# Softmax attention with one head's scores in two halves of 256 queries, and another owner order of the PSUM banks

## The chip, the cores and the metric

The kernel runs on one core of a Trainium2 chip. The metric is the time of one execution in device microseconds (us); shorter is better. PE is the matmul engine (PEld its weight loads), ACT the engine of exponentials and copies, DVE and POOL the vector engines, SP the engine whose queue issues the DMAs.

## The reference

Two attentions over the same 2048 tokens of width 448, 16 heads of 28 each, mixed by a gate. `a` is a linear attention with a learned feature map; `b` is plain softmax attention, and the change lies in `b`:

```
g = sigmoid((x * gate_w).sum(-1))
phi = concat(softmax(p), softmax(-p)) of p = q @ w_phi and k @ w_phi
a = (phi_q (phi_k^T v)) / (phi_q (phi_k^T 1) + 1e-6) @ wo_a
scores = einsum("bhqd,bhkd->bhqk", q, k) * 28**-0.5
b = softmax(scores) @ v @ wo_b
out = g * a + (1 - g) * b
```

All inputs and outputs are float32.

## The kernel before

The first 360 us or so make the projections, all of `a`, and the row maxima of the first queries. Then the softmax attention runs in steps. A step `s` is one group of four heads (of 4 groups), one block of 512 queries (of 4) and one tile of 128 keys (of 16): 256 steps, the first of which is made earlier (`first_scores`). The loop at the end of the kernel calls `scores(s, ...)` and then `values(s - 2)`: the value matmuls of a step come two steps after its scores.

A head has 28 rows of q and k, so four heads lie in four row groups of 32 of PE's array, and matmuls of different heads may run side by side. The operands are kept as a high and a low part, and a score tile of 128 keys by 512 queries is the sum of three passes (`PASSES`, `score`): high by high, low by high, high by low. One of the spare rows of the operands carries the row maximum of the query, so that the exponential of the tile is already the shifted one.

The row maxima of later queries are found ahead, three in a step (`mx_next`, 704 in all): `mx_score` makes a plain score tile of 128 queries by 512 keys of one head, and `mx_done` lets DVE reduce it to a maximum per query. `todo` is the list of these three; its fourth column is the head. In the step's own list l0 and l1 are the heads of the first two, and e0 and e1 the two others, in an order that the third row maximum sets.

Each score tile and each row maximum's tile takes one PSUM bank. Seven banks (`free`) go round: a step with three row maxima takes all seven, four for scores (`st`) and three for maxima (`pm`), and the list `free` is left in the order in which the next step will take them. A bank's next writer on PE waits until ACT (for scores) or DVE (for maxima) has read it. The eighth bank (`pv`) collects the values.

Engines work their instructions in the written order. PE's order in a step of before is, by rounds: e0, e1, maximum of l0, maximum of l1; e0, e1, l0, l1; e0, e1, l0, l1; l0, l1; third maximum, which uses e0's row group; then eight value matmuls (L975). ACT makes four exponentials of 512 columns (L838) in the order e0, e1, l0, l1, each into its own tile of 16 (four steps' worth). DVE makes three reductions (L295).

Of the kernel before, what the change touches and what calls it, by code (L numbers as in the profile page):

```python
# [8 lines left out]
F32 = mybir.dt.float32  # L9
F32R = mybir.dt.float32r  # L10
U32 = mybir.dt.uint32
AF = mybir.ActivationFunctionType
# [5 lines left out]
P = 128  # L18
# [7 lines left out]
NQ = S // 512  # L26
SCALE = DH ** -0.5
# [14 lines left out]
def gated_mix_kernel(ctx, tc, xT, wqkB, wvB, wvA, wkAT, wqAT, phi, woA, woB,  # L42
# [7 lines left out]
    nc = tc.nc  # L50
# [18 lines left out]
    def ps_mx(nm):  # L69
        return ps.tile([P, 512], F32, tag="mx", name=nm, bufs=psn[1])  # L70
# [214 lines left out]
    def mx_score(item, pm):  # L285
        gq, kb, qt, j, _ = item
        js = slice(32 * j, 32 * j + DH)
        nc.tensor.matmul(pm, mxs[("qc", gq)][js, qt * P:(qt + 1) * P],  # L288
                         mxs[("kc", gq // NQ, kb)][js, :], start=True, stop=True,
                         tile_position=(32 * j, 0))  # L290

    def mx_done(item, pm):
        gq, kb, qt, h, col = item
        g, qb = divmod(gq, NQ)
        nc.vector.tensor_reduce(part[:, col:col + 1], pm, AX.X, ALU.max)  # L295
        if h < 3:
            return
        if kb == 1 and qt == 0 and gq + 1 < NG * NQ:
            mx_query(gq + 1)
        if qb == NQ - 1 and g + 1 < NG:  # L300
            if qt == 2 and kb == 3:
                mx_load(g + 1, 0)
            if qt == 3 and kb < 3:
                mx_load(g + 1, kb + 1)
        if qt == 3 and kb == 3:
            mx_reduce(gq)
# [374 lines left out]
    for i in range(2 * NT + 11):  # L681
        t, q = i, i - NT
# [106 lines left out]
    at = ctx.enter_context(tc.tile_pool(name="at", bufs=1, side="right", reuse_waits="tile"))  # L789
    qst_of, kst_of = {}, {}  # L790
# [31 lines left out]
    pv_of, pts, late, mids = {}, {}, {}, {}  # L822
    PASSES = ((0, 0), (1, 0), (0, 1))

    def score(s, j, n, st):

        gq, kt = divmod(s, NT)
        k, q = PASSES[n]
        js = slice(32 * j, 32 * j + 32)
        nc.tensor.matmul(st[j], kst_of[(gq // NQ, kt // 4)][js, k, (kt % 4) * P:(kt % 4 + 1) * P],  # L830
                         qst_of[gq][js, q, :], start=n == 0, stop=n == 2,
                         tile_position=(32 * j, 0), skip_group_check=True)

    def exps_of(s, js, st, pool, **kw):
        pts[s] = {}
        for j in js:
            p = pts[s][j] = pool.tile([P, 512], F32, name=f"p{s}_{j}", **kw)
            nc.scalar.activation(p, st[j], AF.Exp, scale=SCALE)  # L838

    def first_scores():  # L840
        st = [ps_mx(f"st0_{j}") for j in range(4)]
        for n in range(3):
            for j in range(4):
                score(0, j, n, st)
        exps_of(0, range(4), st, at)

    def scores(s, todo):

        if len(todo) == 3:
            l0, l1, e0 = [x[3] for x in todo]
            e1, = {0, 1, 2, 3} - {l0, l1, e0}
            b = free[:]
            free[:] = [b[2], b[0], b[3], b[1], b[6], b[4], b[5]]
            b = [bank(i, f"g{s}_{n}") for n, i in enumerate(b)]
            st, pm = {e0: b[0], e1: b[1], l0: b[4], l1: b[5]}, [b[2], b[3], b[6]]
            for n in range(4):
                for j in (e0, e1) if n < 3 else ():
                    score(s, j, n, st)  # L860
                for i, j in enumerate((l0, l1)):
                    if n:
                        score(s, j, n - 1, st)
                    else:
                        mx_score(todo[i], pm[i])
            mx_score(todo[2], pm[2])
            js = (e0, e1, l0, l1)
        else:
            js = range(4)
            n = 4 + len(todo)  # L870
            b = free[:n]
            free[:] = free[n:] + b[4:] + b[:4]
            b = [bank(i, f"g{s}_{n}") for n, i in enumerate(b)]
            st, pm = dict(enumerate(b[:4])), b[4:]
            for n in range(3):
                for j in js:
                    score(s, j, n, st)
            for x, m in zip(todo, pm):
                mx_score(x, m)
        exps_of(s, js, st, late_p, tag="p", bufs=16)  # L880
        for x, m in zip(todo, pm):
            mx_done(x, m)
# [10 lines left out]
    for t in range(8, NT):  # L893


        if t < NT - 1:
            value_b(t, lambda i: mx_unit() if (11 * (t - 8) + i + 1) * rest // 77
                    > (11 * (t - 8) + i) * rest // 77 else None)
        else:
            value_b(t, lambda i: first_scores() if i == 4 else None)  # L900
        take_acts()
        if t in (8, 12):
            load_k(0, t // 12)
# [10 lines left out]
    free = [0, 1, 2, 3, 4, 5, 6]  # L914

    def bank(i, nm):
        return ps2.tile([P, 512], F32, tag=f"g{i}", name=nm, bufs=1)
# [187 lines left out]
    for s in range(NS + 18):  # L1105
        gq, kt = divmod(s, NT)
# [17 lines left out]
        if 0 < s < NS:  # L1124
            if s in mids:
                mids.pop(s)()
            scores(s, mx_next())
# [83 lines left out]
```

## Time and profile before

| what | before |
|---|---|
| median of 3 runs | 987.37 us (986.72 to 989.15) |
| the profiled execution | 986.75 us |
| its span in the trace | 985.0 us |
| PE, ACT, DVE busy | 99%, 76%, 74% |
| PE's granted clock | full all through |

A row of a group has the line, the engine, the operation, output and input tile by the program's names with their shapes, and the count; behind the bar the busy time in us and the mean of one in ns; behind the second bar the engine's idle time just before such instructions and what ended it. A row of the timeline has the start and the length in us, then the same names; equal neighbours are merged, so that the length runs from the first one's start to the last one's end. Matmul ends are modelled and instructions of one engine overlap, so starts are the safer numbers. Timeline rows were asked for in narrow windows where single instructions were wanted; a merged row then begins with the first instruction that reaches into the window.

### The profile page before, as it was taken

To read this page: it belongs to the slowest core of one execution; us is meant where nothing else is said; L and a number is where in the kernel's file an instruction comes from. 1 tells how busy PE (TensorE), PEld (TensorE's weight loads), DVE (VectorE), ACT (ScalarE), POOL (GpSimd) and SP (SyncE) were. 2 spreads that over 40 slices of the span, in tenths; PEclk is the share of its full clock that TensorE was granted. 3 is DMA by queue.
4 is the path that set the end of the run, shared out by engine and by line. 5 is a ranking of instruction groups with operands and counts; after the bars stand their busy time and mean duration, and the time that the engine had idled before them with its cause. 6 is when DMAs were issued, how large, how long until landed. Compare 5 with 4: busy or idle time off the path is not lost.

```text
span 985.0 us, 22282 instructions
## 1 busy us (share of the span) xinstructions
PE 979.2 (99%) x8392; PEld 607.2 (62%) x8392; DVE 728.5 (74%) x1335; ACT 752.9 (76%) x1442; POOL 234.8 (24%) x224
## 2 busy tenths in 40 slices
PE   9999999999999999999999999999999999999998
PEld 8877877887777665555555555555555555555555
DVE  5566767899766678888888888888888888885112
ACT  4455655577775689988988988988888898897561
POOL 1135535578734710031011001011001011000010
PEclk9999999999999999999999999999999999999999
DMA  9873010013233233121132121122231223000451
GB/s 304 310 253 116 33 54 32 36 37 98 79 103 112 90 114 127 37 58 46 65 89 73 35 61 48 57 82 71 61 83 50 60 58 84 22 20 31 132 159 57
DMA packets 56140, 84.47 MB, mean 86 GB/s; under 512 B 17217, under 2 KB 23985, under 8 KB 56033
## 3 DMA queue, kind: packets, MB, share of 16 engines
q1 hardware_dynamic: 56032, 83.06, 27.3%
q8 instruction: 66, 1.08, 0.5%
q14 instruction: 42, 0.34, 0.1%
HBM read 54.86 MB, written 27.78 MB: 84 GB/s over the span
## 4 chain that ended last, share of the span: by engine, by line
PE 95%; DVE 3%; issue 1%; ACT 0%; POOL 0%; DVEq 0%; POOLq 0%; ACTq 0%
PE g L830 29%; PE pv L975 26%; PE pqk L109 6%; PE poa L109 4%; PE pk L127 4%; PE pva L127 4%; PE g L288 3%; PE pmd L260 3%; PE pob L109 3%; PE pvb L127 2%; PE pvb L109 2%; PE pq L109 2%; PE pn L507 1%; PE pqk L608 1%; PE pft L495 1%
## 5 line engine op out<-in xcount | busy, mean ns | idle before, releaser
L838 ACT ACTIVATE p<-g 128x512 f32<-128x512 f32 x1020 | 526.1, 607 | 83.9 <-PE g L830 83.1
L295 DVE TENSOR_REDUCE part<-g 128x1 f32<-128x512 f32 x704 | 442.3, 684 | 84.4 <-PE g L288 80.4
L830 PEld LDWEIGHTS g<-qst,kst 32*128 32x128 f32 x3060 | 221.2, 183 | 212.1 <-DVE part L295 194.6
L830 PE MATMUL g<-qst,kst 32*128 32x512 f32 x3060 | 337.9, 420 | 0.1
L975 PE MATMUL pv<-p,vb 128*32 128x512 f32 x2048 | 273.0, 605 | 0.0
L288 PE MATMUL g<-kc,qc 28*128 28x512 f32 x704 | 233.3, 495 | 0.0
L394 POOL TENSOR_TENSOR oUb<-oUb,rsb 128x512 f32<-128x512 f32 x15 | 19.3, 1286 | 490.5 <-DMA rsb<-rdb 458.4
L265 DVE CUSTOM_DVE_ANT_0 rl<-pmb,rl 128x512 f32<-128x512 f32 x160 | 103.2, 682 | 44.0 <-ACT rl L264 44.0
L264 ACT ACTIVATE rl<-pmd 128x512 f32<-128x512 f32 x160 | 87.3, 601 | 31.2 <-PE pmb L260 30.0
L288 PEld LDWEIGHTS g<-kc,qc 28*128 28x128 f32 x704 | 86.5, 182 | 0.2
L975 PEld LDWEIGHTS pv<-p,vb 128*32 128x32 f32 x2048 | 40.7, 108 | 65.9 <-issue 64.6
L109 PE MATMUL pqk<-XH,wB 128*128 128x512 f32 x192 | 59.1, 397 | 0.0
L986 DVE SCALAR_TENSOR_TENSOR acc<-pob,gate,acc 128x448 f32<-128x448 f32 x12 | 8.2, 684 | 54.7 <-PE pob L109 54.7
L546 ACT CAST ev<-pqk 128x512 fp32r<-128x512 f32 x28 | 16.0, 589 | 39.5 <-PE pqk L109 23.0
L109 PE MATMUL poa<-woA_s,oTa 128*128 128x448 f32 x192 | 43.5, 375 | 0.0
L260 PE MATMUL pmb<-kp,qp 28*128 28x512 f32 x160 | 42.1, 496 | 0.4
L547 DVE TENSOR_TENSOR ev<-pqk,ev 128x512 fp32r<-128x512 f32 x28 | 19.0, 690 | 30.9 <-ACT ev L546 30.8
L109 PEld LDWEIGHTS pqk<-XH,wB 128*128 128x128 f32 x192 | 35.5, 188 | 8.5 <-issue 1.5
L260 PE MATMUL pmd<-kp,qp 28*128 28x512 f32 x160 | 39.9, 494 | 0.0
L127 PE MATMUL pk<-wkA_s,XH 128*128 128x448 f32 x128 | 39.4, 382 | 0.0
L109 PEld LDWEIGHTS poa<-woA_s,oTa 128*128 128x128 f32 x192 | 35.0, 189 | 6.3 <-issue 2.9
L127 PE MATMUL pva<-wvA_s,XH 128*128 128x450 f32 x128 | 37.8, 372 | 0.0
(154 smaller groups left out, 1089.2 us busy)
## 6 DMA issues: line engine op xcount, KB each, us to landing
qkd<-ev SPq DMA_DIRECT2D x28, 512.0 KB
qst<-qkd SPq DMA_DIRECT2D x64, 112.0 KB
kst<-qkd SPq DMA_DIRECT2D x64, 112.0 KB
od<-oTb SPq DMA_DIRECT2D x48, 112.0 KB
rsa<-rda SPq DMA_DIRECT2D x8, 512.0 KB
oL<-od SPq DMA_DIRECT2D x8, 512.0 KB
rsb<-rdb SPq DMA_DIRECT2D x15, 256.0 KB
gad<-ga SPq DMA_DIRECT2D x16, 224.0 KB
```

Source lines behind the costliest of these rows:

```text
L109: nc.tensor.matmul(dst, l, r, start=i == 0, stop=i == len(todo) - 1)
L127: nc.tensor.matmul(dst[:, :n], l, r, start=i == 0, stop=i == len(todo) - 1, skip_group_check=True)
L260: nc.tensor.matmul(pm[j], qc[js, qt * P:(qt + 1) * P], kc[js, :], start=True, stop=True, tile_position=(32 * i, 0))
L264: nc.scalar.activation(rl, pm[i], AF.Relu)
L265: nc.vector.tensor_tensor_reduce(rl, pm[2 + i], rl, 1.0, LOWEST, ALU.add, ALU.max, part[:, col + i:col + i + 1])
L288: nc.tensor.matmul(pm, mxs[("qc", gq)][js, qt * P:(qt + 1) * P], mxs[("kc", gq // NQ, kb)][js, :], start=True, stop=True, tile_position=(3 ...
L295: nc.vector.tensor_reduce(part[:, col:col + 1], pm, AX.X, ALU.max)
L394: (nc.gpsimd if n == 1 else nc.vector).tensor_mul(oU, oU, rs)
L547: nc.vector.tensor_sub(e[:, 1, :], pq, f32(e[:, 0, :]))
L830: nc.tensor.matmul(st[j], kst_of[(gq // NQ, kt // 4)][js, k, (kt % 4) * P:(kt % 4 + 1) * P], qst_of[gq][js, q, :], start=n == 0, stop=n == ...
L838: nc.scalar.activation(p, st[j], AF.Exp, scale=SCALE)
L975: nc.tensor.matmul(pv[32 * j:32 * j + 32, :], vb[kt // 8][:, kt % 8, 4 * g + j, :], pt[j], start=kt == 0, stop=kt == NT - 1, tile_position ...
```

## The change

In each step with three row maxima, the scores of e0 are made and exponentiated in two halves of 256 queries: six passes of 256 columns instead of three of 512, two exponentials of 256 instead of one. Both halves lie in one bank and one output tile. PE's order is rewritten around them. The third row maximum now uses e1's row group, so e0 and e1 change names in the first two lines. ACT's order becomes first half of e0, e1, second half of e0, l0, l1. The list `free` leaves the banks in another order: e0 takes the bank of the first row maximum, e1 that of e1, the first two maxima those of the second maximum and of e0, l0 that of l0, l1 that of the third maximum, and the third maximum that of l1. Before, the order was: e0 from the first maximum, e1 from e0, the first two maxima from the second maximum and e1, l0 from the third maximum, l1 from l0, the third maximum from l1. Steps with fewer than three row maxima, and the first one, keep their four whole heads.

```diff
-    def score(s, j, n, st):
+    def score(s, j, n, st, c=slice(0, 512)):
...
-        nc.tensor.matmul(st[j], kst_of[(gq // NQ, kt // 4)][js, k, (kt % 4) * P:(kt % 4 + 1) * P],
-                         qst_of[gq][js, q, :], start=n == 0, stop=n == 2,
+        nc.tensor.matmul(st[j][:, c], kst_of[(gq // NQ, kt // 4)][js, k, (kt % 4) * P:(kt % 4 + 1) * P],
+                         qst_of[gq][js, q, c], start=n == 0, stop=n == 2,
                          tile_position=(32 * j, 0), skip_group_check=True)
     def exps_of(s, js, st, pool, **kw):
         pts[s] = {}
-        for j in js:
-            p = pts[s][j] = pool.tile([P, 512], F32, name=f"p{s}_{j}", **kw)
-            nc.scalar.activation(p, st[j], AF.Exp, scale=SCALE)
+        for j, c in js:
+            if j not in pts[s]:
+                pts[s][j] = pool.tile([P, 512], F32, name=f"p{s}_{j}", **kw)
+            nc.scalar.activation(pts[s][j][:, c], st[j][:, c], AF.Exp, scale=SCALE)
+
+    HALF = slice(0, 256), slice(256, 512)
+
+    def whole(js):
+        return [(j, slice(0, 512)) for j in js]
...
         if len(todo) == 3:
-            l0, l1, e0 = [x[3] for x in todo]
-            e1, = {0, 1, 2, 3} - {l0, l1, e0}
+            l0, l1, e1 = [x[3] for x in todo]
+            e0, = {0, 1, 2, 3} - {l0, l1, e1}
             b = free[:]
-            free[:] = [b[2], b[0], b[3], b[1], b[6], b[4], b[5]]
+            free[:] = [b[2], b[1], b[3], b[0], b[4], b[6], b[5]]
             b = [bank(i, f"g{s}_{n}") for n, i in enumerate(b)]
             st, pm = {e0: b[0], e1: b[1], l0: b[4], l1: b[5]}, [b[2], b[3], b[6]]
-            for n in range(4):
-                for j in (e0, e1) if n < 3 else ():
-                    score(s, j, n, st)
-                for i, j in enumerate((l0, l1)):
-                    if n:
-                        score(s, j, n - 1, st)
-                    else:
-                        mx_score(todo[i], pm[i])
+            score(s, e0, 0, st, HALF[0])
+            score(s, e1, 0, st)
+            mx_score(todo[0], pm[0])
+            mx_score(todo[1], pm[1])
+            score(s, e0, 1, st, HALF[0])
+            for j, n in ((e1, 1), (l0, 0), (l1, 0)):
+                score(s, j, n, st)
+            score(s, e0, 2, st, HALF[0])
+            score(s, e0, 0, st, HALF[1])
+            for j, n in ((e1, 2), (l0, 1), (l1, 1)):
+                score(s, j, n, st)
+            score(s, e0, 1, st, HALF[1])
+            score(s, e0, 2, st, HALF[1])
+            for j in (l0, l1):
+                score(s, j, 2, st)
             mx_score(todo[2], pm[2])
-            js = (e0, e1, l0, l1)
+            js = [(e0, HALF[0])] + whole([e1]) + [(e0, HALF[1])] + whole([l0, l1])
```

More of the change, by code (lines that the diff above doesn't have):

```diff
@@ L844, in first_scores @@
                 score(0, j, n, st)
-        exps_of(0, range(4), st, at)
+        exps_of(0, whole(range(4)), st, at)
     def scores(s, todo):
         if len(todo) == 3:
-            l0, l1, e0 = [x[3] for x in todo]
-            e1, = {0, 1, 2, 3} - {l0, l1, e0}
+            l0, l1, e1 = [x[3] for x in todo]
+            e0, = {0, 1, 2, 3} - {l0, l1, e1}
             b = free[:]
-            free[:] = [b[2], b[0], b[3], b[1], b[6], b[4], b[5]]
+            free[:] = [b[2], b[1], b[3], b[0], b[4], b[6], b[5]]
             b = [bank(i, f"g{s}_{n}") for n, i in enumerate(b)]
             st, pm = {e0: b[0], e1: b[1], l0: b[4], l1: b[5]}, [b[2], b[3], b[6]]
-            for n in range(4):
-                for j in (e0, e1) if n < 3 else ():
-                    score(s, j, n, st)
-                for i, j in enumerate((l0, l1)):
-                    if n:
-                        score(s, j, n - 1, st)
-                    else:
-                        mx_score(todo[i], pm[i])
+            score(s, e0, 0, st, HALF[0])
[13 more added lines that the diff above has]
+                score(s, j, 2, st)
             mx_score(todo[2], pm[2])
-            js = (e0, e1, l0, l1)
+            js = [(e0, HALF[0])] + whole([e1]) + [(e0, HALF[1])] + whole([l0, l1])
         else:
@@ L879, in scores @@
                 mx_score(x, m)
+            js = whole(js)
         exps_of(s, js, st, late_p, tag="p", bufs=16)
```

## The prediction

> **What bounds the kernel now.** I read the page's totals first, then the attention stretch 400 to 900 us by groups and by waits, then one step instruction by instruction.
>
> ```profile
> PE 979.2 (99%) x8392; PEld 607.2 (62%) x8392; DVE 728.5 (74%) x1335; ACT 752.9 (76%) x1442; POOL 234.8 (24%) x224
> ...
> L838 ACT ACTIVATE p<-g 128x512 f32<-128x512 f32 x870 | 449.4, 604 | 51.3 <-PE g L830 50.8 <-PE g L288 0.5
> L295 DVE TENSOR_REDUCE part<-g 128x1 f32<-128x512 f32 x651 | 409.1, 684 | 76.1 <-PE g L288 72.2 <-PE g L830 3.9
> L830 PE MATMUL g<-qst,kst 32*128 32x512 f32 x2610 | 294.1, 419 | 0.0
> ```
>
> A busy PE at 99% says little, since the ends of matmuls are modelled. The counts say more: 2610 score matmuls at 12 a step are 217.5 steps in 500 us, so **2.30 us a step**. ACT waits 51 us of these 500 us for scores, so ACT alone is not the bound either. One step:
>
> ```profile
> 664.65 0.50 PE L830 MATMUL g<-qst,kst 32*128 32x512 f32 x2
> 664.66 0.50 PE L288 MATMUL g<-kc,qc 28*128 28x512 f32 x2
> 665.00 0.51 PE L830 MATMUL g<-qst,kst 32*128 32x512 f32 x4
> 665.23 0.63 PE L830 MATMUL g<-qst,kst 32*128 32x512 f32 x5
> 665.26 1.89 DVE L295 TENSOR_REDUCE part<-g 128x1 f32<-128x512 f32 x3 [0.45 <-PE g L288]
> 665.72 2.06 ACT L838 ACTIVATE p<-g 128x512 f32<-128x512 f32 x4 [0.27 <-PE g L830]
> 665.93 0.64 PE L975 MATMUL pv<-p,vb 128*32 128x512 f32 x4
> ...
> 666.69 0.60 ACT L838 ACTIVATE p<-g 128x512 f32<-128x512 f32 x1
> 666.93 0.50 PE L830 MATMUL g<-qst,kst 32*128 32x512 f32 x2
> 667.27 0.43 PE L830 MATMUL g<-qst,kst 32*128 32x512 f32 x3
> 667.35 0.73 PE L830 MATMUL g<-qst,kst 32*128 32x512 f32 x5
> 667.91 0.39 PE L830 MATMUL g<-qst,kst 32*128 32x512 f32 x1
> 668.26 0.64 PE L975 MATMUL pv<-p,vb 128*32 128x512 f32 x4
> ```
>
> Four heads sit in four row groups and run side by side, so matmuls come in rounds of four: 664.65, 665.00, 665.23. The first round takes 0.34 us, because its weights are loaded with nothing to hide them (0.50 us for one, against 0.39 later); a following round in the same row groups takes 0.23. The third round of e0 and e1 starts at 665.23 and their exponentials at 665.72, 0.49 later. ACT starts one every 0.48 us ((2.06 less 0.61) / 3). The third exponential, that of l0, starts at 666.69 and ends at 667.29; 0.06 later, at 667.35, the first pass of l1 of the next step starts, in the bank that l0 left. It could have started at 667.27, with its round. So l1's chain is 0.08 late: its third pass stands at 667.91, the value matmuls 0.35 later at 668.26, and values take 1.00 (665.93 to 666.93).
>
> The loop: from a step's start to its first exponential 1.07, to l0's exponential 0.97, its length 0.60, release 0.06; in the next step two more passes of l1 0.56, to the values 0.35, values 1.00. That is 4.61 for two steps, **2.30 a step**, the mean above. With no bank late, a fourth round would start 0.23 after 665.23 and the values 0.35 later: 0.58 + 0.23 + 0.35 + 1.00 = 2.16 a step.
>
> **What the change does, and what it does not.** In the changed kernel as built, PE counts its finished work up, and ACT waits for a count. For step 61 the program holds this (mx: row maximum; p0 to p2: the three passes; h0, h1: the halves of e0):
>
> ```
> PE   mx l0 +1 = 3347; mx l1 +1 = 3348
> PE   h0p1 e1p1 l0p0 l1p0 h0p2 h1p0 e1p2 l0p1 l1p1 h1p1: no count
> PE   h1p2 +11 = 3359; l0p2 +1 = 3360; l1p2 +1 = 3361; mx e1 +1 = 3362
> ACT  exp h0 waits 3359; exp e1, exp h1: no wait for PE; exp l0 waits 3360; exp l1 waits 3361
> PE   next step: h0p0 waits for row maximum 1, e1p0 for exp e1, mx l0 for row maximum 2,
>      mx l1 for exp h1, l0p0 for exp l0, l1p0 for row maximum 3, mx e1 for exp l1
> ```
>
> Exp h0 reads columns 0 to 255, ready after h0p2, but it waits for h1p2, the last write into that bank. **The early start isn't there**: h0, e1 and h1 all become free to run together. What is left is a fifth exponential, six short passes for three long ones, and new owners of the banks.
>
> The Trainium skill, "PSUM — Partial Sum Buffer", section "PSUM bank collisions raise a hardware error", says the same from the other side: TensorE may not write a bank while ScalarE reads it, in the same partitions, even at other columns. By that rule no order of these halves could start h0 early while h1 is still written; no run here shows it, and the sum goes by the counts.
>
> **The cost, part by part.** ACT first. No exponential of 256 columns is in the trace; the nearest is a copy of that size out of PSUM:
>
> ```profile
> 277.00 0.39 ACT L498 COPY fT<-pft 112x256 f32<-112x256 f32 x1
> 277.26 0.63 ACT L264 ACTIVATE rl<-pmd 128x512 f32<-128x512 f32 x1
> ...
> L498 ACT COPY fT<-pft 112x512 f32<-112x512 f32 x28 | 15.1, 599 | 0.0
> ...
> L838 ACT ACTIVATE p<-g 128x512 f32<-128x512 f32 x1020 | 526.1, 607 | 83.9 <-PE g L830 83.1
> ```
>
> The next instruction starts 0.26 after it. Bounds: 0.24 (half of 0.48) to 0.39 (no overlap). I take 0.26, since the full-size copies and exponentials agree too (599 ns and 607 ns). So ACT runs h0 0.26, e1 0.48, h1 0.26, and l0 starts 1.00 after h0 instead of 0.97. With its length 0.60 and release 0.06, l0's bank comes free 1.66 after exp h0 starts.
>
> Now PE. Before, l0's bank went to l1 and the first pass of l1 stood behind e0p1 and e1p1; l1 ran on by itself, and e0 was hardly touched. After, l0's bank goes to l0p0, which now waits for the *fourth* exponential. Behind it in PE's order stand l1p0, h0p2, h1p0, e1p2 and the rest: two thirds of e0's work. In the old kernel's case of 667.35 e0 and e1 still had their second passes running. What a held PE costs shows in another step, where the wait was long:
>
> ```profile
> 602.95 0.19 PEld L830 LDWEIGHTS g<-qst,kst 32*128 32x128 f32 x4 [0.24 <-ACT p L838]
> 602.95 0.51 PE L830 MATMUL g<-qst,kst 32*128 32x512 f32 x4
> 603.28 0.41 PE L830 MATMUL g<-qst,kst 32*128 32x512 f32 x2
> 603.55 0.60 ACT L838 ACTIVATE p<-g 128x512 f32<-128x512 f32 x1 [0.16 <-PE g L830]
> ```
>
> No weights are loaded past the held instruction; all four load after the release, so the round takes 0.34 (602.95 to 603.28) and e0's exponential comes 0.60 after its pass instead of 0.49: 0.11 for the bare weight load.
>
> A short pass: by columns 0.12 (half of 0.23), with the next weights loaded behind it. Its floor by loads is seen in matmuls of 128 columns that load 128 columns of weights each:
>
> ```profile
> L1072 PE MATMUL pr<-ident,rw x8: 275/276/377, 973.5 to 974.4; 128*128 128x128 f32 x8
> ...
> 973.80 0.83 PE L1072 MATMUL pr<-ident,rw 128*128 128x128 f32 x6
> ...
> L830 PEld LDWEIGHTS g<-qst,kst 32*128 32x128 f32 x3060 | 221.2, 183 | 212.1 <-DVE part L295 194.6
> ```
>
> At 276 ns for one, (0.83 - 0.28) / 5 = 0.11 from start to start, so a load hides in 0.11. Bounds for a short pass: 0.12 to 0.18 (the recorded length of a weight load, 183 ns). I take 0.12.
>
> From the release R of l0p0: h0p2's weights 0.11, h0p2 streams to 0.23, h1p0 to 0.35. h1p1 stands behind l0p1 and l1p1, which follow l0p0 and l1p0 by 0.34, so h1p1 starts at 0.35 and h1p2 at 0.46. Exp h0 follows a pass of e0 by 0.49 less the 0.12 that this pass is shorter, 0.37: R + 0.84 (0.46 + 0.37, rounded at the end). The loop now closes in a single step:
>
> exp h0 to release 1.66 + release to the next exp h0 0.84 = **2.50 us a step**, 0.20 more than 2.30.
>
> The other limits lie under it. The values follow l1p2 and mx e1 (R + 0.58) by 0.35 and take 1.00, so the next step starts at R + 1.93 and could want l0's bank 0.34 later, at R + 2.27; it comes at R + 2.50. Mx l1 waits for exp h1, free at R + 2.03 (0.84, 0.26 + 0.48, 0.39 for its length, 0.06): 0.10 after the step's start, but 0.47 ahead of the next R, so it costs nothing. Mx e1 waits for exp l1, R + 0.84 + 1.66 + 0.48 = R + 2.98, that is 0.48 after the new R, earlier than its place at 0.58. The third row maximum comes about 0.6 before l1p0 needs it: mx e1 at 0.58, DVE's start 0.60 later (as 664.66 to 665.26), 0.68 for the reduction: R + 1.86. Taking e1 for e0 in it moves one of four passes from one row group to the other, and no DMA: the row maxima keep their order in time, and so do SP's issues. Values of a step read exponentials of two steps earlier, which hides the later end of l1.
>
> ```profile
> L295 DVE TENSOR_REDUCE part<-g 128x1 f32<-128x512 f32 x704 | 442.3, 684 | 84.4 <-PE g L288 80.4 <-PE g L830 3.9
> ```
>
> 704 row maxima in threes make 234 changed steps. 234 x 0.20 = **47 us**. The profiled execution took 986.75 us (span 985.0 and 1.75 around it), 0.6 under the median of the three runs. 985.0 + 47 is a span of 1032; against the median it is 987.4 + 46.8 = **1034 us**.
>
> **The rivals.**
> *The held weights cost nothing* (14%): if h0p2's weights are in place before the release, the chain is 0.11 shorter and the step 2.40: 234 x 0.10 = 23, 1010 us. With a half exponential at 0.24 it would be 2.36, 1001. Against it stand the four loads at 602.95.
> *Short passes of one row group do not overlap their weights* (8%). At 0.18 each, h1p2 starts at R + 0.66, the step is 2.69, 1078 us; with load and pass wholly in line, 0.11 + 0.12 = 0.23 each, h1p2 starts at R + 0.79, 2.82, 1109. Against it: 665.00 to 665.23 is 0.23 in the same row groups, a new load included, where a bare load would make it the 0.34 of the first round. The Trainium skill, "TensorE: Matmul & The Clock Gate", section "The mechanism", states that rule: a weight load overlaps running matmuls only in another row group. This trace disagrees with it by that 0.23.
> *Faster* (5%): exp h0 does start after h0p2. Then ACT is ahead by some 0.3, no bank is late, and PE's own 2.16 decides: 234 x 0.14 = 33 less, 955 us. For it: ACT's 51 us of waiting for scores. Against: the count of 3359.
> *No change* (4%): the swap of banks ends the old loop, and the new one closes in 2.30 as well. The way from R to exp h0 would have to be 0.64 instead of 0.84, so that even four short passes in 0.06 each wouldn't do without the first rival.
>
> **How the numbers follow.** The forecast has 69%, with its own range 1022 to 1050 (0.15 to 0.27 a step: a few hundredths on each of two half exponentials and four short passes). Adding the first rival and part of the way to the second gives 1006 to 1064. About 0.3% (3 us) is what can be told from no change here: faster 5%, within 4%, slower 91%.
>
> **What would show it.** In 400 to 900 us: about 200 steps instead of 217, so 400 exponentials of 256 columns and 600 of 512; the weight loads before l0p0 waiting for ACT some 0.2 a step; four loads together right after that wait; exp h0 0.37 after h1p2, never after h0p2; three exponentials in a row without a gap 0.26, 0.48, 0.26 apart; DVE's share down in proportion to the step. Wrong would be: exp h0 starting while h1's passes run, half exponentials 0.3 or more apart, short passes more than 0.14 apart in one row group, or PE's wait for ACT at another place than l0p0.

## The result, and the profile after

The changed kernel takes 1045.26 us (median of 4 runs, 1044.06 to 1045.8) against 987.46 before: a ratio of 1.0581, 95% interval 1.0563 to 1.0599, 58 us slower. Its profiled execution spans 1042.3 us, 57.3 more than before's 985.0.

From the profile of after, the page's totals:

```profile
PE 1036.1 (99%) x9094; PEld 598.2 (57%) x9094; DVE 729.2 (70%) x1335; ACT 767.4 (74%) x1676; POOL 234.6 (23%) x224
```

The groups of the stretch 400 to 900 us, shapes kept apart:

```profile
L839 ACT ACTIVATE p<-g 128x512 f32<-128x512 f32 x589 | 334.0, 614 | 0.0
L839 ACT ACTIVATE p<-g 128x256 f32<-128x256 f32 x392 | 152.0, 388 | 82.3 <-PE g L830 82.3
L830 PE MATMUL g<-qst,kst 32*128 32x512 f32 x1769 | 315.0, 436 | 0.0
L830 PE MATMUL g<-qst,kst 32*128 32x256 f32 x1180 | 248.5, 316 | 0.0
```

The waits of the same stretch (who waited for whom: us in total, times, the longest):

```profile
ACT p L839 <- PE g L830: 82.3, 196, 0.5
PEld g L830 <- ACT p L839: 59.5, 197, 0.3
```

392 half exponentials are 196 steps in 500 us: 2.55 us a step, where before made 217.5 steps of 2.30. PE's weight loads wait 59.5 us for ACT, once a step, 0.30 each; ACT waits 82.3 us for PE, where before it waited 50.8, and its share of the span falls from 76% to 74% with 234 instructions more. Each waits for the other: that is what a closed loop looks like.

One step of after, put together from narrow windows of the timeline (starts are what counts):

```profile
665.59 0.38 ACT L839 ACTIVATE p<-g 128x256 f32<-128x256 f32 x1 [0.43 <-PE g L830]
665.87 0.59 ACT L839 ACTIVATE p<-g 128x512 f32<-128x512 f32 x1
666.35 0.39 ACT L839 ACTIVATE p<-g 128x256 f32<-128x256 f32 x1
666.61 0.62 ACT L839 ACTIVATE p<-g 128x512 f32<-128x512 f32 x1
667.28 0.20 PEld L830 LDWEIGHTS g<-qst,kst 32*128 32x128 f32 x4 [0.30 <-ACT p L839]
667.29 0.51 PE L830 MATMUL g<-qst,kst 32*128 32x512 f32 x4
667.76 0.27 PE L830 MATMUL g<-qst,kst 32*128 32x256 f32 x1
668.13 0.38 ACT L839 ACTIVATE p<-g 128x256 f32<-128x256 f32 x1 [0.41 <-PE g L830]
```

Exp h0, e1, h1 and l0 start 0.28, 0.48 and 0.26 apart. l0's ends at 667.23 (666.61 + 0.62); 0.05 later PE, which has loaded no weights for 0.30, loads four sets at once. The last short pass of e0, h1p2, starts at 667.76, and the next exp h0 at 668.13, 0.37 behind it. From exp h0 to exp h0 are 2.54 us: 1.64 to the end of exp l0, 0.05 release, 0.47 to h1p2, 0.37 to ACT (each rounded).

### The profile page after: what moved, and what is told of

It is laid out like the page before. It is cut to its first block, busy times and chain, and to the rows that moved or that the text cites. A ratio compares the mean times of both kernels' runs of the same rounds, so it can differ in the third digit from the quotient of the medians.

```text
span 1042.3 us, 23748 instructions
## 1 busy us (share of the span) xinstructions
PE 1036.1 (99%) x9094; PEld 598.2 (57%) x9094; DVE 729.2 (70%) x1335; ACT 767.4 (74%) x1676; POOL 234.6 (23%) x224
## 4 chain that ended last, share of the span: by engine, by line
PE 92%; DVE 3%; DMA 2%; issue 1%; ACT 1%; SPq 0%; DVEq 0%; ACTq 0%
PE g L830 31%; PE pv L989 25%; PE g L288 5%; PE poa L109 4%; PE pqk L109 4%; PE pk L127 4%; PE pva L127 4%; PE pmd L260 3%; PE pob L109 3%; PE pvb L127 2%; PE pvb L109 2%; PE pq L109 2%; PE pn L507 1%; DMA xraw<-in_xT_dram 1%; DMA qkd<-ev 1%; PE pft L495 1%
## 5 line engine op out<-in xcount | busy, mean ns | idle before, releaser
L839 ACT ACTIVATE p<-g 128x256 f32<-128x256 f32 (+1 forms) x1254 | 540.8, 532 | 126.6 <-PE g L830 125.8
L830 PE MATMUL g<-qst,kst 32*128 32x512 f32 (+1 forms) x3762 | 397.1, 391 | 0.4 <-ACT p L839 0.3
L830 PEld LDWEIGHTS g<-qst,kst 32*128 32x128 f32 x3762 | 217.1, 183 | 278.1 <-DVE part L295 192.4
L288 PE MATMUL g<-kc,qc 28*128 28x512 f32 x704 | 264.4, 494 | 0.0
L288 PEld LDWEIGHTS g<-kc,qc 28*128 28x128 f32 x704 | 117.7, 182 | 0.2
```

The source lines that it names most:

```text
L830: nc.tensor.matmul(st[j][:, c], kst_of[(gq // NQ, kt // 4)][js, k, (kt % 4) * P:(kt % 4 + 1) * P], qst_of[gq][js, q, c], start=n == 0, sto ...
L839: nc.scalar.activation(pts[s][j][:, c], st[j][:, c], AF.Exp, scale=SCALE)
```

## The experiments

All are compared with the kernel before, run on the same chip beside them (986.5 to 987.1 us). Where nothing else is said, the diff is against the changed kernel.

**Halves taken out, banks kept.** PE's list has three whole passes of e0 at the places of its first passes, and ACT one exponential.

```diff
-            score(s, e0, 0, st, HALF[0])
+            score(s, e0, 0, st)
...
-            score(s, e0, 1, st, HALF[0])
+            score(s, e0, 1, st)
...
-            score(s, e0, 2, st, HALF[0])
-            score(s, e0, 0, st, HALF[1])
+            score(s, e0, 2, st)
...
-            score(s, e0, 1, st, HALF[1])
-            score(s, e0, 2, st, HALF[1])
...
-            js = [(e0, HALF[0])] + whole([e1]) + [(e0, HALF[1])] + whole([l0, l1])
+            js = whole((e0, e1, l0, l1))
```

> Nothing is halved: e0 has three passes of 512 columns and one exponential again; the new order of the banks and the third row maximum on e1's rows stay. Theory (the loss is the single-step loop: l0's first pass waits for ACT, and e0's short passes stand behind it): with whole heads l0's exponential is the third again and frees the bank about 1.63 us after exp e0 starts; e0's third pass follows l0's first at once, so that the next exp e0 comes 0.60 after the release. 2.23 closes below 2.30, and the two-step loop of before decides again, through l0's three passes in place of l1's: 1.07 + 1.63 + 0.57 + 0.35 + 1.00 = 4.62 for two steps, 2.31 a step, 987 to 991 us. Rival (the new order of the banks is what costs): most of the loss stays, 1030 us or more.

988.53 us, ratio 1.0013 (1.0004 to 1.0022). The new order of the banks and the third row maximum on e1's rows cost 1.5 us between them. The loss is in the halves.

**The banks' order of before, halves kept.**

```diff
-            free[:] = [b[2], b[1], b[3], b[0], b[4], b[6], b[5]]
+            free[:] = [b[2], b[0], b[3], b[1], b[6], b[4], b[5]]
```

> The changed kernel with the banks' order of before (l0 takes the third row maximum's bank, l1 that of l0, e1 that of e0). Theory: l1's first pass now waits for exp l0, and it stands one place behind l0's first pass, with the same four short passes of e0 behind it: the same loop of 1.69 + 0.84 = 2.53 to 2.55 a step, 1040 to 1048 us. Rival (the banks' order costs): back to about 990 us.

1040.69 us, ratio 1.0541 (1.0524 to 1.0559). Now l1's first pass waits for exp l0, with the same four short passes behind it, and nearly the same time comes out, 4.6 us less than with the new order. So it is not the bank as such: whichever first pass waits for exp l0, what stands behind that wait decides. Its waits from 400 to 900 us show PE and ACT waiting for each other once a step:

```profile
ACT p L839 <- PE g L830: 79.5, 197, 0.4
...
PEld g L830 <- ACT p L839: 37.0, 190, 0.2
```

**Short passes, but one whole exponential.**

```diff
-            js = [(e0, HALF[0])] + whole([e1]) + [(e0, HALF[1])] + whole([l0, l1])
+            js = whole((e0, e1, l0, l1))
```

> The changed kernel with its six short passes, but one whole exponential of e0 (four exponentials a step). Theory: exp e0 to the release of l0's bank is 0.06 shorter (1.63 for 1.69), release to the next exp e0 stays 0.84: 2.48 to 2.49 a step, 1029 to 1032 us. So the short passes behind the wait make four fifths of the loss. Rival (the fifth exponential is the loss, ACT being the busiest engine by its own count): back to 990 us.

1030.1 us, ratio 1.0432 (1.0416 to 1.0448). Three quarters of the loss stay without the fifth exponential. So does the wait once a step, PE's part of it at 0.20 each (400 to 900 us):

```profile
ACT p L839 <- PE g L830: 83.8, 200, 0.5
...
PEld g L830 <- ACT p L839: 38.6, 195, 0.2
```

**Whole passes, but two half exponentials**: the passes of the first experiment with the `js` of the changed kernel.

> The changed kernel with whole passes of e0 on PE and its two half exponentials on ACT (both wait for the third pass). Theory: one whole pass stands behind the wait, so the single-step loop is 1.69 + 0.60 = 2.29 and doesn't decide; the two-step loop through l0's three passes is 1.07 + 1.69 + 0.57 + 0.35 + 1.00 = 4.68, 2.34 a step: 993 to 1000 us. Rival (the fifth exponential is a large part of the loss by itself): above 1010 us.

996.49 us, ratio 1.0087 (1.0071 to 1.0103). With the four kernels the two parts can be read as a square (medians in us):

| e0's passes on PE | one exponential of e0 | two halves |
|---|---|---|
| three whole | 988.5 | 996.5 |
| six short | 1030.1 | 1045.3 |

The second exponential costs 8 us beside whole passes and 15 beside short ones; the short passes cost 42 and 49. Beside whole passes the two-step loop decides, which has the added ACT time once in two steps; beside short ones the loop closes in one step and has it in each. The 8 and the 15 fit that factor of two: 234 steps times 0.06, the time added by the two halves, are 14 us. The loop beside whole passes was added up but not followed in its trace.

**Two more short passes ahead of l0's first pass.** Nothing is taken away.

```diff
             score(s, e0, 1, st, HALF[0])
-            for j, n in ((e1, 1), (l0, 0), (l1, 0)):
-                score(s, j, n, st)
+            score(s, e1, 1, st)
             score(s, e0, 2, st, HALF[0])
             score(s, e0, 0, st, HALF[1])
-            for j, n in ((e1, 2), (l0, 1), (l1, 1)):
-                score(s, j, n, st)
+            score(s, l0, 0, st)
+            score(s, l1, 0, st)
             score(s, e0, 1, st, HALF[1])
             score(s, e0, 2, st, HALF[1])
+            for j, n in ((e1, 2), (l0, 1), (l1, 1)):
+                score(s, j, n, st)
```

> The changed kernel with its halves, but two more short passes (third pass of the first half, first pass of the second) issued ahead of l0's first pass, so that two and not four stand behind the wait for exp l0. Theory: release to the next exp h0 falls from 0.84 to about 0.61, that loop to 2.30; the two-step loop through l0's three passes is then 1.07 + 1.69 + 0.57 + 0.35 + 1.00 = 4.68, 2.34 a step: 993 to 1003 us, three quarters of the loss gone with no work taken away. Rival (the extra work itself, short passes and a fifth exponential, costs): no change, 1040 us or more.

997.48 us, ratio 1.0106 (1.0088 to 1.0125). The same instructions in another order on PE give back 48 of the 58 us, to within 1 us of the kernel with whole passes and two exponentials. So the short passes cost next to nothing as work; they cost because they stand behind a wait for ACT. Of the waits from 400 to 900 us, PE's for ACT is gone, and ACT's for PE is down to:

```profile
ACT p L839 <- PE g L830: 45.4, 213, 0.5
```

**All short passes ahead.** e1p2 and all six short passes stand ahead of l0's first pass.

```diff
             score(s, e0, 1, st, HALF[0])
-            for j, n in ((e1, 1), (l0, 0), (l1, 0)):
-                score(s, j, n, st)
+            score(s, e1, 1, st)
             score(s, e0, 2, st, HALF[0])
-            score(s, e0, 0, st, HALF[1])
-            for j, n in ((e1, 2), (l0, 1), (l1, 1)):
+            for n in range(3):
+                score(s, e0, n, st, HALF[1])
+            for j, n in ((e1, 2), (l0, 0), (l1, 0), (l0, 1), (l1, 1)):
                 score(s, j, n, st)
-            score(s, e0, 1, st, HALF[1])
-            score(s, e0, 2, st, HALF[1])
```

> The changed kernel with all of e0's short passes issued ahead of l0's first pass; nothing of e0 stands behind the wait for exp l0. Theory: ACT's loop no longer decides, but l0 and l1 now start behind e0's six short passes (0.70 after the step's start instead of 0.34), and PE's own order makes 0.70 + 2 x 0.23 + 0.35 + 1.00 = 2.52 a step: 1033 to 1043 us; PE waits for ACT nowhere for long. Rival (the more of e0 goes ahead, the better): below the 997 us of the kernel with two passes ahead.

996.35 us, ratio 1.009 (1.0073 to 1.0106): the expectation fell, and not by little. l0 and l1 did not start behind e0. The score matmuls that had started by 0.36 us into a step (first start 663.8):

```profile
L830 PE MATMUL g<-qst,kst x7: 277/387/500, 663.8 to 664.2; 32*128 32x512 f32 x4, 32*128 32x256 f32 x3
```

Three short passes and four whole ones are under way or done. e1 can have no more than two of the four (its first two passes); the others are l0p0 and l1p0, though h1p0, h1p1, h1p2 and e1p2, written ahead of them, have not started. So a matmul that waits for its own row group does not hold back later ones of other row groups. What held back e0 in the changed kernel is only that l0p0 waits for another engine.

**The same on the kernel before**, whose work, banks and exponentials stay; the diff is against before.

```diff
-            for n in range(4):
-                for j in (e0, e1) if n < 3 else ():
-                    score(s, j, n, st)
-                for i, j in enumerate((l0, l1)):
-                    if n:
-                        score(s, j, n - 1, st)
-                    else:
-                        mx_score(todo[i], pm[i])
+            for j in (e0, e1):
+                score(s, j, 0, st)
+            mx_score(todo[0], pm[0])
+            mx_score(todo[1], pm[1])
+            for n in (1, 2):
+                for j in (e0, e1):
+                    score(s, j, n, st)
+            for n in range(3):
+                for j in (l0, l1):
+                    score(s, j, n, st)
```

> The kernel of before, its work, banks and exponentials untouched; only PE's written order differs: after the first round all second and third passes of e0 and e1 stand ahead of the first passes of l0 and l1. Theory (row groups run on by themselves: a matmul waiting for its own row group doesn't hold back later ones of other groups, only a wait for another engine does): l0 and l1 still start 0.34 after the step's start or when their bank comes, the two-step loop of 2.30 stays: 984 to 989 us. Rival (PE starts matmuls strictly in the written order, as the prediction took it): l0 and l1 start behind e0's third pass, 0.58 instead of 0.34, and the step is 0.58 + 2 x 0.23 + 0.35 + 1.00 = 2.39: 1005 to 1012 us.

986.5 us against 986.48, ratio 1.0003 (0.9994 to 1.0012): no difference. One of its rounds:

```profile
665.38 0.45 PE L830 MATMUL g<-qst,kst 32*128 32x512 f32 x4
```

Four matmuls start together at 665.38, the step's second round. Of the passes written behind the first round, the first two are the second passes of e0 and e1, and the next two are their third passes, whose row groups have only now begun the second. So the other two of the four can only be l0p0 and l1p0. Writing a matmul ahead of its row group's turn costs nothing here, and a wait for another engine belongs as late in the list as the work allows.

**A real early start.** The first half's exponential stands in the program right behind h0p2, and h1's passes come last but for the third row maximum.

```diff
     def exps_of(s, js, st, pool, **kw):
-        pts[s] = {}
+        pts.setdefault(s, {})
...
             score(s, e0, 1, st, HALF[0])
-            for j, n in ((e1, 1), (l0, 0), (l1, 0)):
-                score(s, j, n, st)
+            score(s, e1, 1, st)
             score(s, e0, 2, st, HALF[0])
-            score(s, e0, 0, st, HALF[1])
-            for j, n in ((e1, 2), (l0, 1), (l1, 1)):
+            exps_of(s, [(e0, HALF[0])], st, late_p, tag="p", bufs=16)
+            for j, n in ((l0, 0), (l1, 0), (e1, 2), (l0, 1), (l1, 1)):
                 score(s, j, n, st)
-            score(s, e0, 1, st, HALF[1])
-            score(s, e0, 2, st, HALF[1])
             for j in (l0, l1):
                 score(s, j, 2, st)
+            for n in range(3):
+                score(s, e0, n, st, HALF[1])
             mx_score(todo[2], pm[2])
-            js = [(e0, HALF[0])] + whole([e1]) + [(e0, HALF[1])] + whole([l0, l1])
+            js = whole([e1]) + [(e0, HALF[1])] + whole([l0, l1])
```

> The changed kernel, but the first half's exponential is written into the program right behind the first half's third pass, and the second half's three passes come after everything but the third row maximum. Exp h0 then waits for the first half alone, and the second half's first pass waits for exp h0 to have read the bank. Theory (an early start in a shared bank is paid by PE): exp h0 starts 0.72 after the step's start instead of 1.07, but the second half can't begin before it ends, at 1.15; three short passes, the third row maximum, 0.35 and the values' 1.00 make 2.7 to 2.8 a step: 1080 to 1100 us. Rival (the late start of exp h0 is the loss): at or below the 987 us of before.

1105.15 us, ratio 1.1193 (1.1176 to 1.1209): the worst of all, 5 us beyond the expected range. One step, from narrow windows:

```profile
664.91 0.50 PE L830 MATMUL g<-qst,kst 32*128 32x256 f32 x2
665.25 0.40 PE L830 MATMUL g<-qst,kst 32*128 32x512 f32 x4
665.75 0.38 ACT L839 ACTIVATE p<-g 128x256 f32<-128x256 f32 x1 [0.36 <-PE g L830]
666.18 0.18 PEld L830 LDWEIGHTS g<-qst,kst 32*128 32x128 f32 x1 [0.50 <-ACT p L839]
666.18 0.38 PE L830 MATMUL g<-qst,kst 32*128 32x256 f32 x1
666.41 0.28 PE L830 MATMUL g<-qst,kst 32*128 32x256 f32 x1
666.53 0.27 PE L830 MATMUL g<-qst,kst 32*128 32x256 f32 x1
667.73 0.50 PE L830 MATMUL g<-qst,kst 32*128 32x256 f32 x2
```

Exp h0 does start early, 0.84 after the step's start (before: 1.07). It ends at 666.13, and only then, at 666.18, may h1 write into the same bank; PE has loaded no weights for 0.50 by then. The three passes of h1 start at 666.18, 666.41 and 666.53. The step is 2.82 long (664.91 to 667.73). The 0.12 beyond the expected 0.72 is between h0p2, in the round of 665.25, and exp h0: 0.50 instead of 0.37. In the written order the whole pass e1p1 stands ahead of h0p2 and starts in the same round, and 0.49 is what a whole pass takes to reach ACT. That completions are counted in the written order, even where starts are not, would explain it; it wasn't tested by itself. The halves share one bank in every run here, so what an early start would bring with two banks stays open.

## Why the prediction was right, point by point

**The sign and the place: right.** The early start isn't there: exp h0 follows h1p2 by 0.37 as forecast (667.76 to 668.13), never h0p2. In the early-start run PE leaves the bank alone until ACT has read the other half, and its weight loads wait 0.50 us for it. The rule quoted from the Trainium skill, "PSUM — Partial Sum Buffer", section "PSUM bank collisions raise a hardware error", asks for just that; it is the program's own wait that keeps the two apart, and no run let them meet.

**The loop: right, and its size 0.05 us too small.** The forecast was 1.66 from exp h0 to the release and 0.84 from there to the next exp h0, 2.50; the step shown has 1.69 and 0.84, together 2.54 before rounding, and the mean is 2.55 (500 us in 196 steps). The terms that were mis-sized:

- exp h0 to exp e1: 0.28, taken as 0.26. The copy of 256 columns that gave 0.26 followed another copy at once. Exp h0 is the first after a pause; the next half, h1, which isn't, gives the 0.26 (666.35 to 666.61). Whole exponentials of the kernel before have the same difference: 0.49 to the next for the first of a step, which comes after a pause, 0.48 otherwise.
- the length of exp l0: 0.62, taken as 0.60.
- 2.55 against 2.54: in the trace of after, 17 of the 195 steps between 400 and 900 us are 2.63 long, the others 2.53 to 2.56. In the 17, l1p0's weights load 0.07 after l0p0's instead of with them. These steps come 16 or 4 apart, as new blocks of queries and keys do; that a wait for their arrival holds l1p0 was not tested.

234 steps times 0.25 (2.55 less 2.30) are some 58 us; the forecast had 0.20 and 47.

**The working inside that 0.84: a right number with a wrong reason.** The prediction, like the section on the kernel before, had PE start matmuls in the written order, so that h1p1 stood behind l0p1 and l1p1. The runs with e0 ahead show that PE doesn't do that across row groups. Short passes of one row group simply follow each other, in the early-start run 0.22 behind the first with its bare weight load and then 0.12 (666.18, 666.41, 666.53, each rounded). By that count too h1p2 starts 0.47 after the release: 0.01 for the place of h0p2, 0.22, 0.12 and 0.12. The two reasons give the same 0.46 and 0.47 here. They come apart when e0 is moved ahead, and there the expectation built on the written order (1033 to 1043) failed against 996.

**The held weights: right.** Four sets are loaded together after the wait (667.28 x4), none before, and the wait is 0.30 a step where some 0.2 was forecast; the step with 2.40, the first rival, did not come.

**Weight loads of one row group**, the second rival, would have given 2.69 to 2.82. It did not come. Short passes 0.12 apart, each with its own weights, leave no room for a load in line of 0.11 beside the pass. The Trainium skill, "TensorE: Matmul & The Clock Gate", section "The mechanism", has weight loads overlap running matmuls only in another row group; the traces disagree by that 0.12, as the trace of before did.

**No cost of the banks' order and of the third row maximum: right with whole heads**, 1.5 us. Beside the halves the order of the banks does show: with that of before the time is 4.6 us less (1040.69 against 1045.26), and in that trace all steps from 400 to 900 us are 2.52 to 2.55 long, none 2.63.

## What to carry to other kernels

Find the wait for another engine in a queue and ask which work behind it that other engine needs next: here four short matmuls behind one wait turned a loop of two steps into a loop of one, and moving two of them ahead gave back 48 of 58 us without taking any work away. A tile split in halves whose dependency is kept for the whole buffer starts no sooner when the second half is written ahead of the first half's reader; written behind the reader, the second half waits for it, and that kernel took 118 us more than before. Read the counts in the built program before believing in the overlap. Where a busy engine waits for a second one and the second waits for the first, look for the closed loop and add it up, not for the busier of the two.

## What the runs showed of the hardware that was not expected

PE starts a matmul of a free row group ahead of earlier ones in the written order that wait for their own row group: l0p0 and l1p0 started in the second round with four matmuls that are written ahead of them still waiting, and the kernel before with e0 and e1 written first ran in 986.5 us against 986.48. The Trainium skill, "TensorE: Matmul & The Clock Gate", section "The mechanism", has starts and ends in strict program order; for starts these runs disagree. For ends the early-start run fits it, in this one arrangement: exp h0 came 0.50 after a short pass with a whole pass written ahead of it, where 0.37 is what a short pass takes.

An exponential of 256 columns out of PSUM frees ACT for the next one after 0.26 us, 0.28 when it is the first after a pause, against 0.48 for 512: the two halves cost 0.06 more than one whole (0.28 and 0.26 less 0.48).
